# Order of weight and batch-1 loads, place of batch 1's key mixing, and filler matmuls in a block-sorted attention with a gated feed-forward layer

## The chip, the cores and the metric

The kernel runs on one core of a Trainium2 chip. The metric is the device time of one execution in microseconds (us). Five runs of the kernel before gave 255.43 to 259.31 us, median 256.12. A traced execution shows each engine's instructions: TensorE (PE, its weight loads as PEld), VectorE (DVE), ScalarE (ACT), GpSimd (POOL) and SyncE (SP), and the 16 DMA engines.

## The reference

Inputs are float32: q, k, v of 4 batches x 8 heads x 768 positions x 64, a `sort_net` of 8 x 8 per batch and head, and the weights of a gated feed-forward layer (512 to 1536 and back).

```
P = sort_net                       # per batch and head, 8 x 8
5 times: P = exp(P - max); P /= row sums; P /= column sums
k_sorted[i] = sum_j P[i, j] k_block[j]      # blocks of 96 positions
v_sorted[i] = sum_j P[i, j] v_block[j]
attn = softmax(q_block[i] @ k_sorted[i].T / 8); o = attn @ v_sorted[i]
x = o as (3072 tokens, 512)        # heads side by side
g = x @ w_gate;  val = x @ w_val
out = (g * sigmoid(g) * val) @ w_out
```

## The kernel before, in words

All matmuls are bf16; the loads from DRAM convert. Feed-forward work is cut into eight passes of 384 tokens, `ffn(0)` to `ffn(7)` (line 563): pass n is half n % 2 of batch n // 2. A pass has 12 gate groups (`gate`, line 353) and 12 value groups (`value`, line 371), each of four accumulating 128x384 matmuls, and, from the second pass on, three output groups for the pass before (`outp`, line 385), each of 12 matmuls of 128x512 in three parts of four. ACT takes the tanh of a gate group (line 365), DVE makes the gated product (lines 367 and 380).

Attention of the batches runs between these groups. For a batch:
- key mixing (`kq_chunk`, line 230): the tile `kq` of a batch holds keys in partitions 0 to 63 and queries in 64 to 127, so each of its matmuls reads both. A second-pass chunk of `kqs` (line 543) is 64 matmuls: 16 columns into PSUM pair "b", drained by DVE, and 16 into pair "a", drained by ACT. Three chunks make a batch.
- value mixing (`v_chunk`, line 241): the values are first copied to `vch`, transposed inside a partition (`copy_v`, line 113). For batch 1 POOL does so in four copies (line 577), each for a quarter of the positions, so every chunk of value mixing needs all four. The chunks (`vs`, line 547) alternate between pairs "b" (drained by ACT) and "a" (drained by DVE).
- units (`units`, line 527): scores, exponentials, attention times values, transposes.

Batch 0 runs ahead of the passes, written out by hand (lines 456 to 475 for its mixing). Some 128x512 matmuls there read a zeroed tile and write a bank that nobody reads (`fill`, line 416).

What sets the order: PE, POOL, DVE and ACT run in the order in which the code issues instructions; from pass 0 on only PE and POOL do, and a scheduler places the others. `merge` (line 550) walks a pass's groups, adds up their stated costs (0.65 for a gate or value group, 0.87 for a part of an output group), and puts in a side piece once the sum has reached the piece's stated time.

All large loads go through POOL's one queue, in the order of lines 136 to 146: two copies for batch 0, a copy that waits for batch 0's last keys (line 139), then the first five 256-column pieces of the gate and value weights (ten transfers of 256 KB), batch 1's keys, batch 1's queries, the sixth pieces, batch 1's values, and `w_out`. Behind them come the keys of batches 2 and 3 (line 575), the copies of batch 1's values, the values of batches 2 and 3 and two casts of queries. The gate group m reads piece m // 2.

Of the kernel before, what the change touches and what calls it, by code (L numbers as in the profile page):

```python
# [17 lines left out]
def kernel(  # L18
# [15 lines left out]
    C = S // NB  # L34
# [5 lines left out]
    DF = moe_w_gate.shape[1]  # L40
# [43 lines left out]
    def kq_tile(b):  # L84
        if b not in kq_tiles:
            kq_tiles[b] = natp.tile([128, C, D], BF16, name=f"kq{b}", tag="nat")
        return kq_tiles[b]

    def load_k(b, lo, hi):
        nc.gpsimd.dma_start(out=kq_tile(b)[0:R, lo:hi, :], in_=k_nat[b, :, lo:hi, :])  # L90
# [6 lines left out]
    def load_q(b, lo, hi):  # L97
        nc.gpsimd.dma_start(out=kq_tile(b)[R:2 * R, lo:hi, :], in_=q_nat[b, :, lo:hi, :])

    def load_v(b, lo, hi):  # L100
        if b // 2 not in v_tiles:
            v_tiles[b // 2] = vnp.tile([128, C, D], BF16, name=f"v{b // 2}", tag="vn")
        u = b % 2
        nc.gpsimd.dma_start(out=v_tiles[b // 2][u * R:(u + 1) * R, lo:hi], in_=v_nat[b, :, lo:hi, :])

    def load_w(sb, dram, lo, hi):
        nc.gpsimd.dma_start(out=sb[:, :, lo:hi], in_=dram[:, :, lo:hi])  # L107

    def load_gv(lo, hi):
        load_w(wg_sb, wg_dram, lo, hi)  # L110
        load_w(wv_sb, wv_dram, lo, hi)
# [25 lines left out]
    copy_v(nc.gpsimd, 0, lowr, 3)  # L137
    landed = const.tile([R, 1], BF16)
    nc.gpsimd.tensor_copy(landed, kq_tiles[0][0:R, C - 1, D - 1:D])
    for m in range(0, 1280, 256):  # L140
        load_gv(m, m + 256)
    load_k(1, 0, C)
    load_q(1, 0, C)
    load_gv(1280, DF)
    load_v(1, 0, C)
    nc.gpsimd.dma_start(out=wo_sb, in_=wo_dram)

    rmix = {b: const.tile([128, 2, 2, H2, NB], BF16, name=f"rmix{b}") for b in (0, 1, "p")}
# [8 lines left out]
    def vt_tile(pair):  # L157
        if pair not in vts:
            t = vtp.tile([C, 2, H * NB, D + 1], BF16, name=f"vt{pair}", tag="vt")
            nc.vector.memset(t[:, :, :, D:D + 1].rearrange("p u n e -> p (u n) e"), 1.0)  # L160
            vts[pair] = t
        return vts[pair]
# [18 lines left out]
    def bank_tile(name, tag="gen"):  # L181
        return psum.tile([128, 512], FP32, name=name, tag=tag, bufs=3 if tag == "gen" else 1)
# [29 lines left out]
    def drain(eng, dst, src):  # L212
        if eng == "v":
            nc.vector.tensor_copy(dst, src)  # L214
        else:
            nc.scalar.copy(dst, src)  # L216
# [10 lines left out]
    def chunk_tile(name, n, tag):  # L227
        return pair_tile(name, tag) if n == 2 else bank_tile(name, tag)
# [12 lines left out]
    def v_chunk(b, at, n, eng, tag):  # L241
        rows = slice(0, 128) if b % 2 else lowr
        dst = vt_tile(b // 2)[:, b % 2]
        mix = vmix[b // 2][rows, b % 2].rearrange("p a b -> p (a b)")
        tp = chunk_tile("tv", n // 8, tag).rearrange("p (l n) -> p l n", n=H * NB)
        for ld in range(n):
            col = (at + ld) * C
            nc.tensor.matmul(tp[:, ld, :], lhsT=vch[rows, col:col + 128], rhs=mix,  # L248
                             start=True, stop=True)
        drain(eng, dst[:, :, at:at + n], tp[0:C].transpose([0, 2, 1]))  # L250
# [14 lines left out]
    def scores(b, u, tag):  # L265
        half, g = divmod(u, H2)
        k_sb, k_at, q_sb, q_at = ((kqts[b], 0, kqts[b], GI * C) if b < 2 else
                                  (kqts["p"], (b - 2) * GI * C, kqts["q"], (b - 2) * GI * C))
        if tag == "gen":
            wide = None  # L270
            pss = [bank_tile("qk"), bank_tile("qk")]
        else:
            wide = pair_tile("qk", tag).rearrange("p (two n) -> p two n", two=2)
            pss = [wide[:, 0], wide[:, 1]]
        for i4 in range(4):
            at = (g * NB + half * 4 + i4) * C
            for two in range(2):
                lo = two * D
                nc.tensor.matmul(pss[two][:, i4 * C:(i4 + 1) * C],  # L279
                                 lhsT=k_sb[lo:lo + D, k_at + at:k_at + at + 128],  # L280
                                 rhs=q_sb[lo:lo + D, q_at + at:q_at + at + C],
                                 start=True, stop=True)
        return wide, pss

    def exps(b, u, wide, pss):
        n = ecount[0] % 8
        ecount[0] += 2
        if wide is None:
            for two in range(2):
                nc.scalar.activation(e_all[:, n + two, 0:4 * C], pss[two][0:C, 0:4 * C], AF.Exp, scale=scale)  # L290
        else:
            nc.scalar.activation(e_all[:, n:n + 2, 0:4 * C], wide[0:C, :, 0:4 * C], AF.Exp, scale=scale)  # L292
        es[(b, u)] = [e_all[:, n, :], e_all[:, n + 1, :]]

    def qk(b, u, tag="b"):
        exps(b, u, *scores(b, u, tag))
# [29 lines left out]
    def xtr(b, u):  # L326
        half, g = divmod(u, H2)
        if g == 0:
            xts[(b, half)] = xtp.tile([128, H2, TW], BF16, name=f"xt{b}_{half}", tag="xt")
        x_ps = xt_tile("x", 1)[:, 0]  # L330
        x_to(x_ps, b, u)
        return xts[(b, half)][:, g, :], x_ps.rearrange("p a b -> p (a b)")

    def x_dma(b, u):
        half, g = divmod(u, H2)
        if g == 0:
            xts[(b, half)] = xtp.tile([128, H2, TW], BF16, name=f"xt{b}_{half}", tag="xt")
        nc.sync.dma_start_transpose(out=xts[(b, half)][:, g, :].rearrange("p (i c) -> p i c", c=C),
                                    in_=sts.pop((b, u)).rearrange("p i two d -> p (i two d)"))
# [74 lines left out]
    idle_ps = bank_tile("idle_ps", "x")  # L414

    def fill(tile, n):
        for _ in range(n):
            nc.tensor.matmul(tile, lhsT=warm_sb[:, 0:128], rhs=warm_sb, start=True, stop=True)
# [37 lines left out]
    fill(idle_ps, 2)  # L456
    v_chunk(0, 0, 8, "v", "gen")
    v_chunk(0, 8, 16, "s", "a")
    v_chunk(0, 24, 16, "v", "b")
    v_chunk(0, 40, 8, "s", "gen")  # L460
    v_chunk(0, 48, 8, "v", "gen")
    v_chunk(0, 56, 8, "s", "gen")
# [17 lines left out]
    idle_ps = bank_tile("idle_ps")  # L480
# [46 lines left out]
    def units(b, us, ats):  # L527
        us = list(us)
        todo = []
        for n, at in enumerate(ats):  # L530
            u, u2 = us[2 * n:2 * n + 2]
            held = []
            todo.append((at, lambda u=u, u2=u2, held=held: (qk(b, u, "b"), held.append(scores(b, u2, "a")))))
            todo.append((at + 1.3, lambda u2=u2, held=held: exps(b, u2, *held[0])))
            for w, tag, t in ((u, "b", 1.9), (u2, "a", 3.6)):
                if b < 2:
                    todo.append((at + t, lambda w=w, tag=tag: av(b, w, tag)))
                    todo.append((at + t + 3.1, lambda w=w: drain("v", *xtr(b, w))))
                else:
                    todo.append((at + t, lambda w=w, tag=tag: (av(b, w, tag), x_dma(b, w))))  # L540
        return todo

    def kqs(b, ats):
        return [(at, lambda n=n: (kq_chunk(b, n * 32, 16, "v", "b"), kq_chunk(b, n * 32 + 16, 16, "s", "a")))
                for n, at in enumerate(ats)]

    def vs(f, size, ats):
        return [(at, lambda m=m: f(1, m * size, size, "sv"[m % 2], "ba"[m % 2])) for m, at in enumerate(ats)]

    def merge(main, side):  # L550
        done, k = 0.0, 0
        side = sorted(side, key=lambda t: t[0])
        for c, f in main:
            f()
            done += c
            while k < len(side) and side[k][0] <= done:
                side[k][1]()
                k += 1
        while k < len(side):
            side[k][1]()  # L560
            k += 1

    def ffn(n):
        todo = []
        for m in range(NFC):
            if n > 0 or m > 1:
                todo.append((0.65, lambda m=m: gate(n, m)))
            if n > 0 or m > 0:
                todo.append((0.65, lambda m=m: value(n, m)))
            if n > 0 and m % 4 == 3:  # L570
                for part in range(3):
                    todo.append((0.87, lambda m=m, part=part: outp(n - 1, m // 4, part)))
        return todo
# [6 lines left out]
    q_cast(2)  # L580
    q_cast(3)
    both = slice(0, 128)
    kq1 = kqs(1, (11.8, 1.3, 5.2))
    merge(ffn(0), units(0, range(4, 8), (0.0, 5.6)) + kq1[:1])
    merge(ffn(1), kq1[1:] + vs(v_chunk, 16, (7.6, 8.4, 9.2, 10.0)) + units(1, range(4), (10.3, 15.0)))
    for s in range(4):
        copy_v(nc.gpsimd, 1, both, s)
    nc.vector.memset(kqt_tile("p")[:, 2 * GI * C:], 0.0)
# [42 lines left out]
```

## Time and profile before

| | |
|---|---|
| runs of the kernel before | 255.43 to 259.31 us, median 256.12 |
| the profiled execution: its time, and its span from first to last instruction | 255.97 us, 254.0 us |
| TensorE busy | 238.1 us, 94% of the span |
| DVE, ACT, POOL busy | 159.4, 110.3, 51.9 us |
| granted TensorE clock | 1.00 |
| longest wait of TensorE for a weight piece | 1.5 us |
| POOL's wait for batch 1's values | 13.6 us |

In the profile, a line names the source line, the engine, the operation and its tiles (out<-in), how many instructions it stands for and their time. `[0.67 <-DMA x]` says that the engine stood idle for 0.67 us just before, and what ended that. Lists of waits give the total in us, how often, and the longest. Lists of transfers give the size of one and the us from issue to landing. A row of stretches gives for each engine the busy time in the stretch and its instructions, then the granted TensorE clock (1.00 is full), the DMA share and GB/s.

### The profile page before, as it was taken

To read this page: it belongs to the slowest core of one execution; us is meant where nothing else is said; L and a number is where in the kernel's file an instruction comes from. 1 tells how busy PE (TensorE), PEld (TensorE's weight loads), DVE (VectorE), ACT (ScalarE), POOL (GpSimd) and SP (SyncE) were. 2 spreads that over 40 slices of the span, in tenths; PEclk is the share of its full clock that TensorE was granted. 3 is DMA by queue.
4 is the path that set the end of the run, shared out by engine and by line. 5 is a ranking of instruction groups with operands and counts; after the bars stand their busy time and mean duration, and the time that the engine had idled before them with its cause. 6 is when DMAs were issued, how large, how long until landed. Compare 5 with 4: busy or idle time off the path is not lost.

```text
span 254.0 us, 6030 instructions
## 1 busy us (share of the span) xinstructions
PE 238.1 (94%) x2545; PEld 143.2 (56%) x2570; DVE 159.4 (63%) x342; ACT 110.3 (43%) x187; POOL 51.9 (20%) x46
## 2 busy tenths in 40 slices
PE   5688998799799999999999999999999999999994
PEld 5275555565555655667656556555655565555543
DVE  6778689684658767558676468546754675546600
ACT  2976652335641643445545424352535253332411
POOL 7848430299559100000000000000000000000000
PEclk9999999999999999999999999999999999999999
DMA  6949999999999168101102111111111111101122
GB/s 105 211 82 161 196 224 207 198 228 224 196 149 158 41 127 169 41 3 41 44 15 75 57 34 57 58 44 32 59 57 41 34 57 57 44 0 41 44 82 85
DMA packets 37866, 23.98 MB, mean 94 GB/s; under 512 B 26064, under 2 KB 34000, under 8 KB 37328
## 3 DMA queue, kind: packets, MB, share of 16 engines
q0 software_dynamic: 21328, 14.16, 38.2%
q1 hardware_dynamic: 16512, 9.45, 13.0%
q8 instruction: 20, 0.33, 0.5%
q14 instruction: 6, 0.05, 0.1%
HBM read 28.32 MB, written 7.86 MB: 142 GB/s over the span
## 4 chain that ended last, share of the span: by engine, by line
PE 72%; DMA 14%; POOL 7%; DVE 3%; issue 2%; ACT 1%; POOLq 0%; DVEq 0%
PE o_ps L392 22%; PE v_ps L375 20%; PE g_ps L357 20%; DMA wv_sb<-in_moe_w_val_dram 10%; DMA kq<-in_k_dram 4%; POOL vch L120 4%; PE av_ps L306 2%; PE qk L279 2%; PE tkq L236 2%; PE tv L258 1%; DVE h L380 1%; PE o_ps L408 1%; POOL wg_sb L107 1%; PE tv L248 1%; POOL wv_sb L107 1%
## 5 line engine op out<-in xcount | busy, mean ns | idle before, releaser
L367 DVE SCALAR_TENSOR_TENSOR gs_sb<-th_sb,g_ps 128x384 bf16<-128x384 bf16 x96 | 52.8, 550 | 55.0 <-ACT th_sb L365 52.8
L375 PE MATMUL v_ps<-xt,wv_sb 128*128 128x384 bf16 x380 | 77.3, 326 | 1.8 <-DMA wv_sb<-in_moe_w_val_dram 1.5
L357 PE MATMUL g_ps<-xt,wg_sb 128*128 128x384 bf16 x376 | 76.5, 325 | 0.8 <-DMA wg_sb<-in_moe_w_gate_dram 0.7
L365 ACT ACTIVATE th_sb<-g_ps 128x384 bf16<-128x384 f32 x96 | 47.1, 490 | 57.9 <-PE g_ps L357 55.3
L392 PE MATMUL o_ps<-wo_sb,h 128*128 128x512 bf16 x256 | 62.0, 379 | 1.1
L380 DVE SCALAR_TENSOR_TENSOR h<-v_ps,gs_sb 128x384 bf16<-128x384 f32 x96 | 53.3, 555 | 8.1 <-PE v_ps L375 1.3
L375 PEld LDWEIGHTS <-wv_sb 128*128 128x128 bf16 x380 | 35.5, 97 | 25.1 <-DMA wv_sb<-in_moe_w_val_dram 1.9
L357 PEld LDWEIGHTS <-wg_sb 128*128 128x128 bf16 x376 | 34.6, 97 | 24.1 <-DMA wg_sb<-in_moe_w_gate_dram 0.8
L392 PEld LDWEIGHTS <-h 128*128 128x128 bf16 x276 | 26.3, 98 | 28.2
L397 ACT COPY o_sb<-o_ps 128x512 f32<-128x512 f32 x23 | 13.5, 585 | 53.1 <-PE o_ps L392 53.1
L120 POOL COPY vch<-v 64x1536 bf16<-64x1536 bf16 (+1 forms) x10 | 28.0, 2841 | 19.9 <-DMA v<-in_v_dram 19.9
L292 ACT ACTIVATE e_all<-qk 96x768 bf16<-96x768 f32 x30 | 22.6, 803 | 7.6 <-PE qk L279 7.6
L312 DVE TENSOR_TENSOR st<-av_ps,r_sb 96x512 bf16<-96x512 f32 x32 | 21.7, 679 | 0.2
L306 PEld LDWEIGHTS <-e_all 96*128 96x128 bf16 x256 | 12.3, 98 | 5.1 <-ACT e_all L292 0.9
L306 PE MATMUL av_ps<-vt,e_all 96*128 96x65 bf16 x256 | 13.5, 194 | 0.2 <-ACT e_all L292 0.2
L214 DVE CAST vt<-tv 96x1024 bf16<-96x1024 f32 (+1 forms) x9 | 9.8, 1100 | 4.7 <-PE tv L248 4.7
L216 ACT CAST vt<-tv 96x1024 bf16<-96x1024 f32 (+1 forms) x9 | 9.0, 1030 | 3.8 <-PE tv L258 2.6
L310 DVE RECIPROCAL r_sb<-av_ps 96x8 f32<-96x8 f32 x32 | 6.4, 199 | 6.2 <-PE av_ps L306 6.2
L216 ACT CAST kqt<-tkq 128x1024 bf16<-128x1024 f32 (+1 forms) x7 | 6.0, 894 | 7.3 <-PE tkq L236 7.3
L236 PE MATMUL tkq<-rmix,kq 128*64 128x64 bf16 x384 | 7.7, 197 | 0.6 <-issue 0.5
L214 DVE CAST kqt<-tkq 128x1024 bf16<-128x1024 f32 (+1 forms) x7 | 7.4, 1067 | 0.9 <-PE tkq L236 0.8
L236 PEld LDWEIGHTS <-kq 128*64 128x64 bf16 x384 | 6.8, 112 | 2.0 <-issue 1.9
(79 smaller groups left out, 134.1 us busy)
## 6 DMA issues: line engine op xcount, KB each, us to landing
out_dram<-o_sb SPq DMA_DIRECT2D x23, 256.0 KB, 2.0
v<-in_v_dram POOLq DMA_DIRECT2D x3, 768.0 KB, 11.4
kq<-in_q_dram POOLq DMA_DIRECT2D x2, 768.0 KB, 12.7
wg_sb<-in_moe_w_gate_dram POOLq DMA_DIRECT2D x6, 256.0 KB, 8.7
wv_sb<-in_moe_w_val_dram POOLq DMA_DIRECT2D x6, 256.0 KB, 9.2
wo_sb<-in_moe_w_out_dram POOLq DMA_DIRECT2D x1, 1536.0 KB, 24.3
kp<-in_k_dram POOLq DMA_DIRECT2D x2, 768.0 KB, 27.5
q_scr<-in_q_dram POOLq DMA_DIRECT2D x2, 768.0 KB, 17.7
```

The lines of the kernel that those rows point to most:

```text
L120: eng.tensor_copy(dst, src.transpose([0, 2, 1]))
L214: nc.vector.tensor_copy(dst, src)
L236: nc.tensor.matmul(tp[two * D:(two + 1) * D, lc, :], lhsT=kq_tiles[b][:, at + lc, :], rhs=rm[:, two, :], start=True, stop=True)
L292: nc.scalar.activation(e_all[:, n:n + 2, 0:4 * C], wide[0:C, :, 0:4 * C], AF.Exp, scale=scale)
L306: nc.tensor.matmul(o[:, two, i4, :], lhsT=e[:, i4 * C:i4 * C + 128], rhs=vt[:, 2 * g + two, half * 4 + i4, :], start=True, stop=True)
L312: nc.vector.tensor_tensor(st.rearrange("p i two d -> p two i d"), o[0:C, :, :, 0:D], r_sb.to_broadcast([C, 2, 4, D]), op=ALU.mult)
L357: nc.tensor.matmul(g_ps, lhsT=wg_sb[:, kc, ts(m, 128)], rhs=xt[:, kc, :], start=(kc == 0), stop=(kc == NKC - 1))
L365: nc.scalar.activation(th_sb, g_ps, AF.Tanh, scale=0.5)
L367: nc.vector.scalar_tensor_tensor(gs_sb, th_sb, 1.0, g_ps, op0=ALU.add, op1=ALU.mult)
L375: nc.tensor.matmul(v_ps, lhsT=wv_sb[:, kc, ts(m, 128)], rhs=xt[:, kc, :], start=(kc == 0), stop=(kc == NKC - 1))
L380: nc.vector.scalar_tensor_tensor(h_tiles[n][:, m, :], v_ps, 0.5, gs_tiles.pop(m), op0=ALU.mult, op1=ALU.mult)
L392: nc.tensor.matmul(o_ps, lhsT=h_w[:, m, ts(t3, 128)], rhs=wo_sb[:, m, :], start=(m == 0), stop=(m == NFC - 1))
```

## The change

```diff
@@ loads on POOL's queue (lines 140 to 146)
-    for m in range(0, 1280, 256):
+    for m in range(0, DF, 256):
         load_gv(m, m + 256)
     load_k(1, 0, C)
+    load_v(1, 0, C)
     load_q(1, 0, C)
-    load_gv(1280, DF)
-    load_v(1, 0, C)
     nc.gpsimd.dma_start(out=wo_sb, in_=wo_dram)
@@ mixing of batch 0 (lines 456 to 462)
     v_chunk(0, 0, 8, "v", "gen")
     v_chunk(0, 8, 16, "s", "a")
+    fill(idle_ps, 2)
     v_chunk(0, 24, 16, "v", "b")
+    fill(idle_ps, 2)
     v_chunk(0, 40, 8, "s", "gen")
@@ first two passes (lines 583 to 585)
-    kq1 = kqs(1, (11.8, 1.3, 5.2))
-    merge(ffn(0), units(0, range(4, 8), (0.0, 5.6)) + kq1[:1])
-    merge(ffn(1), kq1[1:] + vs(v_chunk, 16, (7.6, 8.4, 9.2, 10.0)) + units(1, range(4), (10.3, 15.0)))
+    merge(ffn(0), units(0, range(4, 8), (0.0, 5.6)))
+    merge(ffn(1), kqs(1, (0.3, 2.6, 4.9)) + vs(v_chunk, 16, (6.2, 7.3, 8.4, 9.5)) + units(1, range(4), (11.0, 15.6)))
```

All twelve pieces of the gate and value weights (range end `DF` is 1536) are issued ahead of batch 1's keys; batch 1's values come between its keys and its queries. On TensorE, the first chunk of batch 1's key mixing stood behind value group 10 of the first pass and now stands behind gate group 0 of the second; the other two stood behind value groups 0 and 3 of the second pass and now stand behind value groups 1 and 3. The first chunk of batch 1's value mixing stood behind the first output group and now stands behind two of its three parts, the second behind the third part, the third behind gate group 4, the fourth behind gate group 5. The first score pair of batch 1 stood directly behind the fourth chunk and now has value group 5 and gate group 6 ahead of it. Four more filler matmuls stand in batch 0's value mixing. No transfer changes its size.

## The prediction

> **What bounds the kernel now.** I read five views in this order: the page's head, TensorE's waits, TensorE's order of time around those waits, the order of time of POOL (its queue issues every load), and the landing of single transfers. The page's head first:
>
> ```profile
> span 254.0 us, 6030 instructions
> PE 238.1 (94%) x2545; PEld 143.2 (56%) x2570; DVE 159.4 (63%) x342; ACT 110.3 (43%) x187; POOL 51.9 (20%) x46
> ```
>
> TensorE is busy for 94% of the span, so a change can gain only where TensorE stands still. Its waits, longest first (total, times, longest), without the first ten us:
>
> ```profile
> PE v_ps L375 <- DMA wv_sb<-in_moe_w_val_dram: 1.5, 1, 1.5
> PE qk L279 <- DVE vt L214: 1.4, 1, 1.4
> PE g_ps L357 <- DMA wg_sb<-in_moe_w_gate_dram: 0.7, 1, 0.7
> ...
> PE tv L248 <- POOL vch L120: 0.3, 1, 0.3
> ```
>
> All four lie between 42 and 67 us. Together they are 1.50 + 1.36 + 0.67 + 0.34 = 3.87 us, the most that this change could take away on TensorE. The order of time of TensorE there (start, duration; in brackets the idle time before and what ended it):
>
> ```profile
> 41.85 0.81 PE L375 MATMUL v_ps<-xt,wv_sb 128*128 128x384 bf16 x4
> 42.50 0.34 PE L323 MATMUL x_ps<-ident,st 96*128 96x96 bf16 x4
> 43.51 0.82 PE L357 MATMUL g_ps<-xt,wg_sb 128*128 128x384 bf16 x4 [0.67 <-DMA wg_sb<-in_moe_w_gate_dram]
> 45.84 0.82 PE L375 MATMUL v_ps<-xt,wv_sb 128*128 128x384 bf16 x4 [1.50 <-DMA wv_sb<-in_moe_w_val_dram]
> 46.59 1.20 PE L236 MATMUL tkq<-rmix,kq 128*64 128x64 bf16 x64
> ...
> 57.10 2.76 PE L392 MATMUL o_ps<-wo_sb,h 128*128 128x512 bf16 x11
> 60.20 0.64 PE L248 MATMUL tv<-vmix,vch 128*128 128x64 bf16 x16 [0.34 <-POOL vch L120]
> ...
> 66.65 0.34 PE L279 MATMUL qk<-kqt 64*128 64x96 bf16 x8 [1.36 <-DVE vt L214]
> 66.92 0.82 PE L357 MATMUL g_ps<-xt,wg_sb 128*128 128x384 bf16 x4
> ```
>
> A gate or value group of four matmuls advances TensorE by 0.65 us (start to start), a kq chunk of 64 by 1.13 (50.63 to 51.76). The last weight pieces come late because POOL issues them behind batch 1's keys and queries:
>
> ```profile
> 25.03 0.54 POOL L90 DMA_DIRECT2D kq<-in_k_dram  x1 [0.97 <-DMA wg_sb<-in_moe_w_gate_dram]
> 26.36 0.54 POOL L98 DMA_DIRECT2D kq<-in_q_dram  x1 [0.78 <-DMA wv_sb<-in_moe_w_val_dram]
> ...
> 29.05 0.75 POOL L107 DMA_DIRECT2D wv_sb<-in_moe_w_val_dram  x1 [0.56 <-DMA wv_sb<-in_moe_w_val_dram]
> 30.82 0.54 POOL L104 DMA_DIRECT2D v<-in_v_dram  x1 [1.02 <-DMA wg_sb<-in_moe_w_gate_dram]
> ...
> 48.92 11.22 POOL L120 COPY vch<-v 64x1536 bf16<-64x1536 bf16 x4 [13.62 <-DMA v<-in_v_dram]
> ```
>
> Each issue here waits for the landing of an older weight piece, never for a younger transfer. The view of transfers, asked for windows with one issue each, gives us from issue to landing:
>
> ```profile
> kq<-in_q_dram POOLq DMA_DIRECT2D x1, 768.0 KB, 16.0
> v<-in_v_dram POOLq DMA_DIRECT2D x1, 768.0 KB, 18.1
> ```
>
> Issue plus this: k1 lands at 37.9, q1 at 26.36 + 16.0 = 42.4, the last gate piece at 43.4, the last value piece at 45.8, v1 at 30.82 + 18.1 = 48.9, w_out at 56.2. The fifth value piece landed at 34.5. They land in the order of issue, back to back: what is ahead of a transfer in bytes sets when it lands.
>
> **The change part by part.**
>
> *Load order.* No transfer is added or resized, and the issue slots stay where they are, since each waits for one of the first ten weight pieces, which do not move. The last two pieces (512 KB together) now follow the fifth value piece directly: pieces at the full rate come 1.3 to 1.5 us apart, so they land near 36 and 37.5. TensorE wants them at 42.8 and later, so the waits of 0.67 and 1.50 us go. Then k1 (near 41), v1 (between 44.4 and 45.8; I take 45), and q1 last. Ahead of q1 and including it there are now just the bytes that before ended with v1, so q1 lands where v1 did: 48.9, or up to 0.7 earlier because the hand-overs between 512-byte and 12-KB packets are fewer, or up to 0.6 later by a straggling engine (the wv piece landed 2.4 after the wg piece, where 1.3 is usual). I take 48.6, bounds 48.2 and 49.5. w_out behind it has the same bytes ahead: 56.2 at the latest.
>
> *Key mixing in the second pass.* The first of the three kq chunks moves from behind value group 10 of the first pass to behind gate group 0 of the second. It reads k1 and q1 (one tile, both halves). TensorE reaches it thus: 42.84 (start of gate 10 without its wait) + five groups of 0.65 (gate 10, value 10, gate 11, value 11, gate 0) + 0.17 of transposes = 46.26, and at most 0.86 later with the fills. q1 is not there: TensorE stands still from about 46.3 to 47.1 until 48.65. So the removed wait of 2.17 us is replaced by a new one of 1.5 to 2.4 us, 3 us later in the order. What is queued behind it: all of TensorE; DVE and ACT run dry too, so nothing else is late for it.
> From 48.65: three chunks 3.39 + seven groups (value 0 to value 3) 4.55 = 7.94. In before the same stretch (46.59 to 57.10) held 3 chunks, 10 groups and a transpose, 10.06, and took 10.51; I add 0.25 of that 0.45 slack. The first output group starts at 56.85 instead of 57.10: gain 0.25 (bounds: 0.8 gained, where w_out at 56.2 caps it; 0.65 lost).
>
> *Value mixing.* POOL's four copies start when v1 lands, 45 instead of 48.9, and end 11.2 later, at 56.2 (bounds 55.6 and 57.0). The first chunk of value mixing now stands behind two thirds of the output group: 56.85 + 8 x 0.216 (twelve take 2.59 in the chain of waits at 224.61) = 58.6. The copies are done: 0.34 us gained. Behind the last chunk there was the score pair, whose second half reuses the bank that DVE drains (vt, 65.38 to 66.59): 1.36 us. Now value 5 and gate 6 (1.30 us) lie between. DVE first does gate 5's product, so its 1.22 us drain ends near 65.1 where TensorE wants the bank at 64.9: 0.3 stays (bounds 0 and 0.6). Gain 1.06. The third kq drain (DVE 1.22, from 56.65) ends near 57.9, ahead of 58.6, so it costs nothing; cover lost, it would cost 0.7.
>
> *Fills.* Four more 128x512 matmuls in batch 0's value mixing, whose result nobody reads: at 0.21 us each (five took 1.25), 0.86 us of TensorE. They push drains of value mixing by 0.4 on DVE and up to 0.7 on ACT, all of the first pass with them. Bounds: 0.86 lost and nothing. I take nothing, since the first pass ends in the wait for q1, which has 1.5 us of slack; gone that wait, they cost 0.5 to 0.9. A gain from them is not excluded either (below), but the granted clock is 1.00 in every stretch already.
>
> *After 67 us* the order differs only in where a few small groups stand; POOL is free 4 us earlier, which brings batch 2 and 3's values and q casts forward; they had 30 us to spare. Nothing.
>
> Sum against the profiled execution, 255.97 us with a span of 254.0: 0.25 + 0.34 + 1.06 = 1.65, to which I add half of the 0.25 slack that I booked, 0.12: -1.8. The profiled run lies 0.15 below the median of the runs shown (256.12), so the median goes to 254.3.
>
> **A rule weighed.** In the stretch from 8 to 10 us TensorE was busy for 0.18 us only, with the idle stretch of 1.82 us its longest once warm, and the granted clock was still 1.00 afterwards:
>
> ```profile
> 8.00:10.00 2.00, 0.18 (x2) 0.07 (x1) 1.45 (x7) 1.90 (x5) 2.00 (x2) 1.00 1.14 242
> ```
>
> The new wait may be 2.4 us, longer than any row covers, so by rows a clock loss behind it is not excluded. The Trainium skill, "TensorE: Matmul & The Clock Gate", Part 1, says the clock falls to half after an idle window of about 3.4 us, free-running; by that rule the wait is too short and the sum stands. By the same rule the fills are paid for nothing, as no gap in the first pass reaches 3.4 us.
>
> **The rivals.**
> - *q1 comes early and w_out is the bound.* If the three 768 KB loads run at k1's 3.4 us each from 37.2, q1 lands at 47.4, TensorE reaches the output group at 55.7 and waits for w_out at 56.2 or, if that too is earlier, 55.5. Then 0.9 to 1.6 there plus 1.4: 2.3 to 3.0 gained, 253.5. For it: k1's own 3.4. Against it: q1 took 4.5 and v1 3.1 behind straggling engines.
> - *The wait eats it.* q1 at 49.5, the score pair still waits 0.6, drains bunch up: 0.65 lost, 1.1 gained: 255.7, no change.
> - *Slower: q1 shares the queue with w_out.* Place: POOL's queue; q1 is issued at 30.82, 1.1 us ahead of the 1536 KB of w_out. If the two went side by side at half rate, q1 would take 7.4 us from 45 instead of 3.7 and land at 52.4: 3.8 later than in my sum, 256.12 - 1.8 + 3.8 = 258.1. It decides from a landing at 50.4. For it: v1's last packets overlapped w_out's first. Against it: every landing above is in order of issue. 1% is passed only with a further half us.
> - *The change doesn't do what it says* (weight waits stay): the wait at 43.5 could only stay if the pieces landed after 42.8, 5 us later than their bytes say.
>
> **How the numbers follow.** My forecast 0.58 (its own range 253.4 to 255.2), early q1 0.17, eaten 0.12, shared queue 0.07, and 0.06 for a loss of clock behind the wait, which no row prices. One per cent, about what a measurement of this kernel can tell from no change, is 2.56 us: faster than 253.56 are two thirds of the second case and the edge of the first, 0.11 + 0.06 = 0.17; slower than 258.7 are half of the shared queue and the loss of clock, 0.035 + 0.06, or 0.10; the rest, 0.73, is the same. The range reaches from the early case (252.9) to beyond the eaten one (256.4).
>
> **What would show it.** Right: no TensorE wait for wg or wv; one wait of 1.5 to 2.4 us of tkq for the q load, ending near 48.6; POOL's copies from 45 to 56; no wait of tv for vch; the score pair's wait below 0.6; every stage after 67 us shifted by 1.6 to 2.2. Wrong: q1 landing past 50 or before 47.5, copies not over at 58.6, a granted clock below 1.00 after the wait, or a first pass that ends later than 47.1 without q1's wait.

## The result, and the profile after

The changed kernel takes 254.18 us (median of 31 runs, 253.44 to 256.53) against 256.3 us for the kernel before (57 runs): a ratio of 0.9924, 95% interval 0.9906 to 0.9942. The forecast was 254.3. The ratios here and below leave out executions more than 1.5% above the fastest of their kernel (one of e1's twelve), so they differ a little from the quotient of the medians printed. The profiled execution took 253.90 us with a span of 251.8, where before it was 255.97 and 254.0.

The page's head and TensorE's waits between 42 and 68 us, after the change:

```profile
span 251.8 us, 6035 instructions
PE 238.2 (95%) x2548; PEld 143.2 (57%) x2574; DVE 159.3 (63%) x342; ACT 110.5 (44%) x187; POOL 51.9 (21%) x46
```

```profile
PE tkq L235 <- DMA kq<-in_q_dram: 1.1, 1, 1.1
PE qk L278 <- DVE vt L213: 0.3, 1, 0.3
```

TensorE does the same work (238.2 us busy, 238.1 before) in a shorter span. Its four waits of 3.87 us in this stretch have become two of 1.14 + 0.26 = 1.40 us. (From the load of w_out to the added fills, lines of the changed kernel count one lower.) The same places in TensorE's order of time:

```profile
46.65 0.81 PE L356 MATMUL g_ps<-xt,wg_sb 128*128 128x384 bf16 x4
48.60 1.20 PE L235 MATMUL tkq<-rmix,kq 128*64 128x64 bf16 x64 [1.14 <-DMA kq<-in_q_dram]
...
56.95 1.90 PE L391 MATMUL o_ps<-wo_sb,h 128*128 128x512 bf16 x7
58.69 0.63 PE L247 MATMUL tv<-vmix,vch 128*128 128x64 bf16 x16
...
65.36 0.35 PE L278 MATMUL qk<-kqt 64*128 64x96 bf16 x8 [0.26 <-DVE vt L213]
65.64 0.82 PE L374 MATMUL v_ps<-xt,wv_sb 128*128 128x384 bf16 x4
```

No gate or value group waits for weights. The wait has moved to the first kq chunk and has the queries' name on it. The output group starts only 0.15 us earlier than before (56.95 against 57.10); nearly all of the gain comes behind it, where value mixing no longer waits and the score pair waits 0.26 us instead of 1.36: value group 6 starts at 65.64, the last line above. Before, it was:

```profile
67.59 0.81 PE L375 MATMUL v_ps<-xt,wv_sb 128*128 128x384 bf16 x4
```

POOL, and the landing of the queries:

```profile
29.57 0.52 POOL L98 DMA_DIRECT2D kq<-in_q_dram  x1 [0.78 <-DMA wg_sb<-in_moe_w_gate_dram]
...
44.38 11.24 POOL L120 COPY vch<-v 64x1536 bf16<-64x1536 bf16 x4 [10.10 <-DMA v<-in_v_dram]
```

```profile
kq<-in_q_dram POOLq DMA_DIRECT2D x1, 768.0 KB, 18.9
```

The queries land at 29.57 + 18.9 = 48.5, where before the values landed (48.9). The copies run from 44.4 to 55.6 instead of 48.9 to 60.1.

### The profile page after: what moved, and what is told of

Same layout as the page of the kernel before. It is cut to its first block, busy times and chain, and to the rows that moved or that the text cites. A ratio compares the mean times of both kernels' runs of the same rounds, so it can differ in the third digit from the quotient of the medians.

```text
span 251.8 us, 6035 instructions
## 1 busy us (share of the span) xinstructions
PE 238.2 (95%) x2548; PEld 143.2 (57%) x2574; DVE 159.3 (63%) x342; ACT 110.5 (44%) x187; POOL 51.9 (21%) x46
## 4 chain that ended last, share of the span: by engine, by line
PE 74%; DMA 15%; DVE 3%; POOL 3%; issue 2%; ACT 1%; DVEq 0%; POOLq 0%
PE o_ps L391 23%; PE v_ps L374 21%; PE g_ps L356 20%; DMA kq<-in_q_dram 8%; DMA kq<-in_k_dram 4%; DMA wg_sb<-in_moe_w_gate_dram 4%; PE tkq L235 3%; PE av_ps L305 2%; PE qk L278 2%; PE tv L257 1%; DVE gs_sb L366 1%; PE o_ps L407 1%; DVE vt L213 1%; POOL wg_sb L107 1%; POOL wv_sb L107 1%
## 5 line engine op out<-in xcount | busy, mean ns | idle before, releaser
L364 ACT ACTIVATE th_sb<-g_ps 128x384 bf16<-128x384 f32 x96 | 47.1, 491 | 58.1 <-PE g_ps L356 54.9
L120 POOL COPY vch<-v 64x1536 bf16<-64x1536 bf16 (+1 forms) x10 | 28.0, 2847 | 18.9 <-DMA v<-in_v_dram 18.9
## 6 DMA issues: line engine op xcount, KB each, us to landing
wo_sb<-in_moe_w_out_dram POOLq DMA_DIRECT2D x1, 1536.0 KB, 24.4
```

Of the source, the lines that this page charges most:

```text
L120: eng.tensor_copy(dst, src.transpose([0, 2, 1]))
L364: nc.scalar.activation(th_sb, g_ps, AF.Tanh, scale=0.5)
```

## The experiments

The theory: three things changed places on one full queue. What comes last on it is waited for, and the gain is the difference between the waits removed and the one made. The rivals were that one part alone carries the gain, that the added fills cost time, and that they matter through TensorE's clock. Each time is a median of 6 to 12 executions; each ratio is to the kernel before on the same chip.

**e1: without the added fills.**

```diff
     v_chunk(0, 8, 16, "s", "a")
-    fill(idle_ps, 2)
     v_chunk(0, 24, 16, "v", "b")
-    fill(idle_ps, 2)
     v_chunk(0, 40, 8, "s", "gen")
```

> The changed kernel without its four added fills. Theory A (the fills' delay of 1.05 us at gate group 2, 30.66 against 29.61, dies in the wait for q1): TensorE reaches the first kq chunk 1.0 to 1.2 us earlier, its wait grows from 1.1 to about 2.2 us, the end does not move: 254.2 us, within 0.3. Rival B (the fills lie on the path): 253.1. Rival C (the fills keep the clock up in some executions): 254.8 or more, or a wider scatter, with a granted clock below 1.00.

Measured: 255.4 us (253.27 to 257.15), ratio 0.9965 (0.9931 to 0.9999). The profiled execution is what theory A says: the wait for the queries is longer (1.78 us, less than the 2.2 expected) and the end the same, 253.84 us against 253.90.

```profile
48.51 1.20 PE L235 MATMUL tkq<-rmix,kq 128*64 128x64 bf16 x64 [1.78 <-DMA kq<-in_q_dram]
```

But that is one of five executions near 253.5, all with a mean granted clock of 0.999 or 1.00. The other seven lie at 255.0 to 257.2, all with 0.987 or 0.993. Of the changed kernel's first 32 executions seven were at 0.992 or 0.993, and took 255.8 to 256.5. So rival C fits the scatter: without the fills the clock is lost more often. That the fills cost nothing e1 doesn't show: its five executions without a loss have a median of 253.47 us, the 25 of the changed kernel's first 32 have 253.98, but were not measured beside them. Nor is the loss new: of the 61 executions of the kernel before that ran beside the experiments, 16 were at 0.985 to 0.993. None of those was profiled, so where they lose it is open. For the changed kernel, e7, e8 and e10 narrow it down.

**e2: only the fills, in the kernel before** (the same two lines added).

> The kernel before with only the four fills added. Theory A: the first pass runs 1.05 us later and the waits for the last weight pieces shrink by that (0.67 to 0, 1.50 to 1.1 us): no change, 256.3 within 0.3. Rival B (the delay is kept to the end): 257.3.

Measured: 256.54 us, ratio 1.0039 (1.0019 to 1.0060). Both theories missed: a loss, but not the whole delay. In its profile the value weights are waited for 1.09 us instead of 1.50, as A says, and the first value-mixing chunk 0.94 instead of 0.34, since the copies end no earlier; the profiled time is 256.33. What makes the rest of the 0.6 us between the medians is open.

**e3: only the new load order.** The loads as in the changed kernel; TensorE's order and the fills as before.

> The kernel before with only the new load order. Theory A: the weight waits are gone, but the first kq chunk, still behind value group 10, is reached near 44.2 and waits 4.3 us for q1 (48.5); from there 10.06 us of work and 0.45 of slack to the first output group at 59.0 (57.1 before), the copies are done (0.34 gained), the score pair keeps its wait: 257.9, that is 1.6 slower. Rival B (the load order alone carries the gain): 254.2 to 255. Rival C (a wait over 3.4 us drops the granted clock, as the Trainium skill says in TensorE: Matmul & The Clock Gate, Part 1): clock below 1.00 behind the wait and 259 or more.

Measured: 260.2 us, ratio 1.0167 (1.0136 to 1.0198): rival B is out, A too small, C right; all six executions are at 0.993 or below. The order of time at the first kq chunk, and the stretch from 49 to 53 us:

```profile
49.41 1.92 PE L235 MATMUL tkq<-rmix,kq 128*64 128x64 bf16 x64 [5.42 <-DMA kq<-in_q_dram]
```

```profile
49.00:53.00 4.00, 3.59 (x73) 2.87 (x74) 1.61 (x3) 1.01 (x1) 4.00 (x2) 0.50 1.25 208
```

The granted clock (third figure from the end) is half, and the chunk takes 1.92 us where it took 1.20. It fell in the wait already (the stretch from 48 to 49 us has 0.65). The load order alone is a loss of 4 us; it pays only together with TensorE's new order.

**e4: only TensorE's new order.** The two `merge` lines as in the changed kernel; loads and fills as before.

> The kernel before with only the new places of the key and value mixing in TensorE's order. Theory A: both weight waits stay (2.2 us), the first kq chunk starts at 48.6 without a wait, the first output group at 57.0, but the copies end at 60.1 as before, so the first value-mixing chunk waits 1.4 us (58.7 to 60.1); the score pair's wait falls to 0.3: 255.7, 0.6 faster. Rival B (the new order alone carries the gain): 254.2.

Measured: 254.85 us, ratio 0.9951 (0.9926 to 0.9977).

```profile
44.98 0.82 PE L375 MATMUL v_ps<-xt,wv_sb 128*128 128x384 bf16 x4 [1.21 <-DMA wv_sb<-in_moe_w_val_dram]
...
59.72 0.64 PE L248 MATMUL tv<-vmix,vch 128*128 128x64 bf16 x16 [1.61 <-POOL vch L120]
```

Both waits are where theory A has them. The values landed 0.5 us earlier than in the profile before (POOL's copies start at 48.41 instead of 48.92), and the path waits for these copies; that is most of why 1.1 us was gained and not the 0.6 expected. In medians the new order alone brings 1.1 us of the change's 2.1. The load order adds to that only with the clock kept: e1, which has both without the added fills, is no better in the ratio (0.9965 against 0.9951, overlapping intervals). Its five executions without a loss took 253.3 to 253.8 us, e4's ten, all without one, 254.2 to 255.3, on the same chip.

**e5: queries ahead of the values.**

```diff
     load_k(1, 0, C)
+    load_q(1, 0, C)
     load_v(1, 0, C)
-    load_q(1, 0, C)
```

> The changed kernel with batch 1's queries loaded ahead of its values. Theory A (one of the two that come last is always waited for): q1 lands near 44.4, no wait at the first kq chunk, which starts near 47.4; the first output group is reached at 56.0 or so, w_out has landed or lands by 56.2; v1 lands near 48.5, the copies end near 59.7, and the first value-mixing chunk waits about 1.9 us (57.8 to 59.7): 1.0 later than the changed kernel's 58.7, so 255.2. Rival B (the swap of v1 and q1 does nothing): 254.2. Rival C (no wait at all any more): 253.2.

Measured: 255.67 us, ratio 0.9959 (0.9931 to 0.9987), as theory A says; its wait is the copies', the first value-mixing chunk starts at 59.62 instead of 58.69, and behind the wait the clock fell in the profiled execution (stretch from 62 to 64 us):

```profile
59.62 0.64 PE L247 MATMUL tv<-vmix,vch 128*128 128x64 bf16 x16 [1.99 <-POOL vch L120]
```

```profile
62.00:64.00 2.00, 2.00 (x23) 1.33 (x20) 1.22 (x1) 0.45 (x2) 2.00 (x2) 0.51 1.01 203
```

**e6: later kq chunks,** `kqs(1, (2.6, 3.9, 5.2))` instead of `(0.3, 2.6, 4.9)`.

> The changed kernel with the first kq chunk two groups later, behind value group 1, and the second behind value group 2; the third stays. Theory A (the wait for q1 is all that the change leaves on the path): TensorE reaches the first chunk at 49.2, q1 is there (48.5), the wait of 1.1 us goes; w_out allows the output group from 55.3 to 56.2, where it was reached at 56.95: 0.75 to 1.1 faster than the changed kernel, 253.2, and no execution below a clock of 0.998. Rival B (the drains of the chunks, now two groups apart, wait on DVE instead): 254.2 or more.

**e7: the same without the four fills.**

> The same later chunks, without the four fills. Theory A (fills matter only by shortening the wait for q1): TensorE reaches the first chunk near 48.2 to 48.4, waits 0.2 to 0.5 us, then meets w_out at 55.3 to 56.2: 253.2, as with the fills, and no execution below 0.998. Rival B (the fills keep the clock up in batch 0's value mixing itself): executions at 0.993 as without the fills before (7 of 12), median 255.

Measured: 253.33 us for e6, ratio 0.988 (0.9843 to 0.9918), and 253.39 us for e7, ratio 0.988 (0.9844 to 0.9916); all twelve executions at 0.998 or more. Theory A holds in both: with the wait for the queries gone (0.61 us of it is left in e7), the fills make no difference. That none of e7's six executions lost clock, with no fills, speaks against its rival B: e1 lost it in 7 of 12. What is left in e6 is a pause in the third chunk, then w_out, in its order of time:

```profile
55.39 0.76 PE L235 MATMUL tkq<-rmix,kq 128*64 128x64 bf16 x37 [0.77 <-issue]
56.31 1.89 PE L391 MATMUL o_ps<-wo_sb,h 128*128 128x512 bf16 x7 [0.15 <-DMA wo_sb<-in_moe_w_out_dram]
```

The pause carries no name ("issue"). A bank still being drained, as e9's expectation has it, it is not: the drains of the second chunk were over at 53.95 (DVE) and 53.71 (ACT). Its cause is open, and it cost next to nothing, since w_out landed at 31.90 + 24.4 = 56.3.

**e8: e1 with the wait filled.**

```diff
+    cover = bank_tile("cover", "x")
-    merge(ffn(1), kqs(1, (0.3, 2.6, 4.9)) + ...
+    merge(ffn(1), [(0.3, lambda: fill(cover, 9))] + kqs(1, (0.3, 2.6, 4.9)) + ...
```

> The changed kernel without the four fills in batch 0's value mixing, but with nine 128x512 fills (1.95 us) directly ahead of the first kq chunk, where TensorE would stand for q1 for 1.8 to 2.2 us. Theory A (an idle TensorE in that wait loses clock in some executions): the same path, the fills end near 48.3 and q1 comes at 48.5, but every execution keeps a clock of 0.998 or more: median 253.8 and a scatter under 1.5 us. Rival B (the clock is lost in batch 0's value mixing, where the four fills were): about half of the executions at 0.993, median 255.4, like the kernel with neither.

Measured: 254.14 us (253.24 to 254.68), ratio 0.9899 (0.9866 to 0.9932).

```profile
46.48 2.11 PE L417 MATMUL cover<-warm_sb 128*128 128x512 bf16 x8
48.70 1.20 PE L235 MATMUL tkq<-rmix,kq 128*64 128x64 bf16 x64
```

The same end, and none of the executions at 255 and above that e1 had. One of six was still at 0.993 (254.12 us), so the wait is not the only place where the clock can be lost; no profile shows that place. One in six against seven in twelve is a small sample, but e6, e7 and e9 point the same way: in their profiles TensorE waits at most 0.61 us for the queries, and none of their 18 executions lost clock.

**e9: the chunks spread,** `kqs(1, (1.9, 3.2, 4.9))`, with the fills.

> The changed kernel with its kq chunks behind gate group 1, gate group 2 and value group 3, so that two and three groups lie between them. Theory A (with the later chunks, what was left was the third chunk's 0.77 us for a bank still being drained, then w_out): the first chunk is reached near 48.6, as q1 lands, the third finds its bank free, and the output group then waits for w_out at 55.5 to 56.2 where it started at 56.3: 0 to 0.7 faster than the later chunks, 253.0, all executions at 0.998 or more. Rival B (w_out was the bound there already): 253.3, the same, with a wait for w_out of 0.5 us or more in place of the bank's.

Measured: 252.71 us (252.25 to 253.72), ratio 0.9853 (0.9820 to 0.9886), six of six at 0.999 or more: faster than both kernels.

```profile
48.26 1.20 PE L235 MATMUL tkq<-rmix,kq 128*64 128x64 bf16 x64
...
53.99 1.23 PE L235 MATMUL tkq<-rmix,kq 128*64 128x64 bf16 x64
55.33 1.90 PE L391 MATMUL o_ps<-wo_sb,h 128*128 128x512 bf16 x8
```

No bracket is left on these lines: the first chunk comes just behind the queries, the third runs without a pause, and the output group starts when w_out lands (31.58 + 23.7 = 55.3; its weight load waits 0.23 us for that). In e6 it also started as w_out landed, at 56.3, so w_out bounds both, as rival B says, though with a shorter wait than the 0.5 us it named. That the spread gains over e6 is not shown: the intervals overlap, and the landing of w_out alone differs by 1.0 us between the two profiles.

**e10: the changed kernel once more.**

> The changed kernel itself once more, on the chip of the run beside it. Theory A: 254.2, within 0.3, with some executions (7 of 32 so far) at a granted clock of 0.993 and 2 us longer, those in which the wait for q1 comes out long. Rival B (those executions were of one chip): none at 0.993.

Measured: 254.25 us (12 executions), ratio 0.9916 (0.9887 to 0.9945); two executions at 0.993, 256.19 and 256.75 us. The first of them is the one profiled, so the same program can be seen with and without the loss. Its order of time, and three stretches:

```profile
49.29 1.42 PE L235 MATMUL tkq<-rmix,kq 128*64 128x64 bf16 x64 [2.31 <-DMA kq<-in_q_dram]
50.64 1.46 PE L374 MATMUL v_ps<-xt,wv_sb 128*128 128x384 bf16 x4
...
59.24 1.90 PE L391 MATMUL o_ps<-wo_sb,h 128*128 128x512 bf16 x8
```

```profile
49.00:51.00 2.00, 1.71 (x66) 1.51 (x67) 0.98 (x1) 0.26 (x1) 2.00 (x2) 0.76 1.25 209
51.00:53.00 2.00, 2.00 (x8) 0.99 (x7) 0.83 (x3) 0.76 (x1) 2.00 (x1) 0.50 1.24 208
55.00:57.00 2.00, 2.00 (x29) 1.25 (x22) 1.53 (x3) 1.41 (x2) 1.71 (x3) 1.00 1.03 215
```

The wait is 2.31 us instead of 1.14, because TensorE comes 0.5 us earlier and the queries 0.7 later. Then the clock is half for some 3.5 us (0.007 of 254.1 us lost, twice that at half speed). From the first chunk to the output group (59.24) it takes 9.95 us instead of 8.35. So of the 2.29 us between the two profiled executions 0.69 is the later landing, and 1.60 the clock.

## Why the prediction was right, point by point

- *Weight waits.* Gone. The last value piece landed at 25.82 + 10.4 = 36.2; forecast 37.5. About half of that difference is chance: batch 0's keys landed earlier, and POOL issued the first weight piece at 15.90 where it was 16.59 before. The prediction had the issue slots stay where they are.
- *The queries land where the values did.* 48.5, forecast 48.6; the chunk started at 48.60, forecast 48.65. In the other profiles with a wait for the queries it started at 48.51 (e1), 48.97 (e7), 49.29 (e10) and 49.41 (e3), all inside the bounds 48.2 to 49.5. That the queries came 0.4 us earlier than the values had is luck, by the earlier start of the queue: from the landing of the fifth value piece it took 15.1 us (33.4 to 48.5), where before it was 14.4 to the values. So the gain that the prediction allowed for fewer hand-overs between packet sizes is not seen in this run, and no run isolates it. e5 is the crosscheck: with the two exchanged, the wait changes its name, and the time goes up by 0.9 us (the ratios 0.9959 and 0.9924, of 256.3; their intervals overlap, but the first value-mixing chunk is 0.9 later in the profile too).
- *Size of the new wait.* 1.14 us, forecast 1.5 to 2.4: TensorE got to the chunk at 47.46, later than the 46.3 to 47.1 of the forecast. The mis-sized term, in this execution, is the fills: they were bounded by 0.86 us, their own time on TensorE. Gate group 2 started 1.05 us later than before (30.66 against 29.61), and the w_ps matmuls ahead of the fills had started 0.16 earlier. So the delay was 1.21 us, and the excess of 0.35 stands in waits ahead of transposes, 0.31 and 0.34 us where before there was one of 0.15. In e10, the same kernel, those waits are missing; TensorE got there at 46.98 and waited 2.31 us, inside the forecast. So the excess is one execution's. In the sum it vanished, as TensorE was early anyway.
- *Output group* 56.95, forecast 56.85. *Copies* done at 55.6, forecast 56.2; the 0.34 us wait is gone. *Score pair* 0.26, forecast 0.3. The three terms of the sum were 0.25, 0.34 and 1.06; the profiles have 0.15, 0.34 and 1.10.
- *Gain.* Value group 6 starts 1.95 us earlier (67.59 to 65.64), and the span ends 2.2 earlier. The forecast was 1.8. In medians the gain is 2.1; the time still came out at 254.2, near the forecast's 254.3, because the median before over more runs is 256.3 and not 256.12. The 0.25 that came after 67 us had been put at nothing; 0.17 of it is a wait of a gate group for DVE at 97.16 that isn't there any more.
- *Fills cost nothing.* Right for the path of the profiled executions, incomplete for the median: with them fewer executions lose clock, and they shorten the wait behind which e10 loses it. The prediction left a gain from them open but gave no price. e1 against the change puts it at about 1 us (the ratios 0.9965 and 0.9924); the intervals just overlap, so the size is uncertain. The share of executions below 0.995 is clearer, 7 of 12 without the fills and 9 of 44 with them.
- *Loss of clock behind the wait,* a rival without a price, and one of the prediction's own signs of being wrong: it does happen. Nine of 44 executions are below 0.995; in the one that was profiled the loss stands behind this wait and costs 1.60 us. It is too rare to move the median: 254.12 us without the nine, 254.19 with them. As the kernel before loses clock in 16 of 61, the change is not shown to make the loss more frequent.

## What to carry to other kernels

On a full queue a reordering doesn't remove the last landing, it gives it to another tile: work out who reads the transfer that is now last, when TensorE gets there, and move that reader behind work that is ready (e9: two more groups of 0.65 us ahead of the first chunk, 1.5 us in the median against e10 on the same chip). A load order and an order of work belong together: here one alone lost 4 us and the other won 1.1. And a wait of two us on TensorE costs more than its length when the clock falls behind it, so look at the granted clock of several executions before a filler matmul is called useless.

## What the runs showed of the hardware that was not expected

The granted clock fell to 0.50 at waits of 1.99 us (e5), 2.31 us (e10) and 5.42 us (e3), and stayed at 1.00 in profiled executions behind 1.14 us (the change) and 1.78 us (e1). At the two shorter waits the fall comes up to a us after the matmuls have started again (in e10 the stretch from 49 to 51 us has 0.76), and lasts some 3.4 us by stretches of 1 us; at the long one it comes in the wait itself (0.65 from 48 to 49 us, with the first matmul at 49.41) and lasts some 6.8. The same kernel has executions with the loss and without it. The Trainium skill, "TensorE: Matmul & The Clock Gate", Part 1, asks for an idle window of about 3.4 us, free-running, before the clock halves, and of about 3.4 us of sustained work before it is full again. The half clock and its length at the short waits agree with the page. The condition doesn't: two waits much shorter than the window were enough, and the measurement decides. The prediction gave both this rule and the row from 8 to 10 us (1.82 us idle, the clock at 1.00 afterwards), and its sum went by the rule; the row, which left a loss behind 2.4 us open, was the better guide.
